# Attention and experts in one program: other blocks' operands stepped at first products only, two weight fetches two steps and one step later

## The chip, the cores and the metric

The kernel runs on one core of a Trainium2 chip. The metric is the device time of one execution in microseconds (us); lower is better. The engines are TensorE (PE, matrix products; its weight loads are PEld), VectorE (DVE), ScalarE (ACT), GpSimd (POOL) and SyncE (SP), which issues most of the transfers.

## The reference

A banded attention feeds a layer of four experts. Heads 0 to 3 look back 32 positions, heads 4 to 7 look back 128 positions in steps of 4. Every token goes through all four experts, weighted by its normalised probabilities.

```python
# q, k, v: (4 batches, 8 heads, 576, 64); x: (2304, 512); w1: (4, 512, 1024); w2: (4, 1024, 512)
scores = scale * np.matmul(q, k.transpose(0, 1, 3, 2))
mask_plain = (rel >= 0) & (rel < window)
mask_dil = (rel >= 0) & (rel < window * dilation) & (rel % dilation == 0)
scores = np.where(masks[None, :, :, :], scores, -1000000000.0)
attn = softmax(scores)
x = np.matmul(attn, v).transpose(0, 2, 1, 3).reshape(B * S, H * D)
p = domain_probs / (domain_probs.sum(-1, keepdims=True) + 1e-09)
for e in range(E):
    h = np.maximum(x @ w1[e], 0.0)
    out += p[:, e:e + 1] * (h @ w2[e])
```

## The kernel before

Everything is fp32. To multiply at the speed of a narrower type, each operand is split into a high part (written by ACT, L113) and the rest (a subtraction on DVE or POOL, L116), and each product is made of three: high by high, rest by high, high by rest.

**The experts.** x is cut into blocks of 384 tokens, numbered i = 0 to 5, and two neighbours make one large block m = 0, 1, 2 of 768 tokens. The 1024 columns of F of each expert are cut into units u of 256 columns. A visit is one pair (u, m); there are 48, some 15.6 us each, and `visits` (L497) lists them: block 0 first, for the units u = 1 to 15, then blocks 1 and 2 for each unit. A visit makes the first product x @ w1 by Strassen-Winograd's scheme, seven products of quarters in place of eight: `mm1_a` (L415) makes two of them and `mm1_b` (L428) five. They need sums of quarters of w1 and of x. Then `mm2` (L463) makes the second product for half 1 of the tokens and afterwards for half 0, three tiles of 128 tokens each; behind every tile DVE adds the weighted tile to `acc` (L488). In between stand two steps of the next visit's `mm1_a`. Banks: `m2` has two for the tiles until the attention is over, then four; `m1x` and `m1y` have one each, then two.

DVE makes L423, L439 and L443 (sums of products), then L406 (the rest parts `hl` of the hidden layer, behind ACT's high parts `hh`, L400), then the three L488 of a half.

**The operands of x.** For a block i, `x_part` (L208) splits one quarter: the high part on ACT, the rest part (`xl_T`, `xl_B`) on POOL if i is even, on DVE if i is odd. `x_sums` (L198) makes the four sums of quarters on DVE, L203, one piece each. They are generators: every piece is one instruction or two.

**The lists.** `queue` holds pieces of the weights and of block 0's x, `later` the pieces of the other blocks' x. `step()` (L569) issues one piece of a list. After each yield of the experts' generator the main loop calls it once or more. `need` (L580) issues all pieces of one kind at once, if they haven't been stepped through yet; so does `need(x_sums, 5)` (L556) in the visit before the last of block 0.

**The attention** is a pipeline of steps of two granules; a granule is one batch, one pair of heads and a third of the sequence. Eight stages run over the granules at different lags, and the experts' visits are woven in behind each step, from step 10 on. SP loads q and k (`q_s`, `k_s`, six buffers each, L245, L246) and the weights (`r`, L98 for w1 and L106 for w2) and, once, the probabilities (`pw`, L737). v is loaded from ACT's queue for the first two batches. `steps` and the fetches at fixed steps (`if n == 4:` and so on) set the order on SP.

Every engine runs its instructions in the order of the program.

Of the kernel before, what the change touches and what calls it, by code (L numbers as in the profile page):

```python
# [21 lines left out]
def band_masks(S):  # L22


    import numpy as np

    masks, which = [], []
    for run in (S, S // DILATION):
        for i in range(S // QB):
            a = (i * QB + np.arange(QB))[:, None]  # L30
            c = (i * QB - WINDOW + np.arange(KB))[None, :]
            seen = (c >= 0) & (a - c >= 0) & (a - c < WINDOW) & (a // run == c // run)
            m = np.where(seen, np.float32(0), np.float32(-8e9))
            same = [j for j, other in enumerate(masks) if np.array_equal(other, m)]
            if not same:
                same = [len(masks)]
                masks.append(m)
            which.append(same[0])
    return np.stack(masks), which
# [3 lines left out]
def kernel(  # L43
# [12 lines left out]
    _, which = band_masks(qT.shape[3])  # L56
    B, NP, _, S = qT.shape
    NT, DM = out.shape
    E, _, F = w1.shape
# [35 lines left out]
    def fetch_w1(u):  # L95
        e, s = divmod(u % NU, FPE)
        r = wp.tile([128, 4, FU], F32, tag="r1", name="r1", bufs=2)
        nc.sync.dma_start(  # L98
            out=r, in_=w1[e, :, s * FU:(s + 1) * FU].rearrange("(c p) f -> p c f", p=128)
        )  # L100
        raw1[u] = r

    def fetch_w2(u):
        e, s = divmod(u % NU, FPE)
        r = wp.tile([128, 2, DM], F32, tag="r2", name="r2")
        nc.sync.dma_start(  # L106
            out=r, in_=w2[e, s * FU:(s + 1) * FU, :].rearrange("(c p) d -> p c d", p=128)
        )
        raw2[u] = r
# [353 lines left out]
    def mm2(k, first, last, half):  # L463
        u, m = k
        e = u // FPE % E
        if first and m not in acc_t:
            if m == NBL - 1:
                pools["late"]()
            acc_t[m] = pools["acc"].tile([128, TB // 128, DM], F32, name=f"acc_{m}")
        for i in range(TH // 128):  # L470
            at = half * (TH // 128) + i
            tt = m * (TB // 128) + at
            acc = acc_t[m][:, at, :]
            po = pools["m2"].tile([128, 512], F32, tag="m2", name="m2")

            cs = range(2) if half == 0 else (1, 0)
            for n, (c, low) in enumerate([(c, low) for low in range(2) for c in cs]):
                h = h_t[k, f"{c + 1}{half + 1}"][low][:, i * 128:(i + 1) * 128]
                for x, w in enumerate(w2_op[u, c][:2 - low]):
                    nc.tensor.matmul(  # L480
                        po, h, w, start=(n == 0 and x == 0), stop=(n == 3)
                    )
            if first:
                nc.vector.tensor_scalar(
                    out=acc, in0=po, scalar1=pn[:, tt, e:e + 1], scalar2=None, op0=ALU.mult
                )
            else:
                nc.vector.scalar_tensor_tensor(  # L488
                    out=acc, in0=po, scalar=pn[:, tt, e:e + 1], in1=acc,
                    op0=ALU.mult, op1=ALU.add,  # L490
                )
            if last:
                nc.sync.dma_start(out=out[tt * 128:(tt + 1) * 128, :], in_=acc)
            yield


    visits = [(u, 0) for u in range(1, NU)]  # L497
# [2 lines left out]
    def experts(begin):  # L500
# [24 lines left out]
        for i, (u, m) in enumerate(visits):  # L525
# [22 lines left out]
            if m == blocks[0]:  # L548
                need(w2_late, u)
            yield from mm2((u, m), *ends, 1)  # L550
            if i + 1 < len(visits):
                begin()
                yield from opening
                if visits[i + 1] == (NU - 1, 0):

                    need(x_sums, 5)  # L556
                    for n in ("T2", "T1"):
                        for j in (4, 5):
                            prepare(x_part, j, n)
            yield from mm2((u, m), *ends, 0)  # L560
            if m == blocks[-1] and u + 2 <= LAST:
                prepare(w2_late, u + 2)
# [3 lines left out]
    queue = []  # L566
    later = []

    def step(of=None):  # L569
        of = queue if of is None else of  # L570
        while of:
            if next(of[0][1], 0) != 0:
                return
            of.pop(0)

    def prepare(what, *args, soon=False, of=None):
        of = queue if of is None else of
        of.insert(0 if soon else len(of), ((what, args), what(*args)))
# [11 lines left out]
    with tc.manual_schedule():  # L590
# [58 lines left out]
        def weigh():  # L649

            nc.vector.reduce_sum(out=ps_, in_=pw, axis=mybir.AxisListType.X)
            nc.vector.tensor_scalar(
                out=ps_, in0=ps_, scalar1=1e-9, scalar2=None, op0=ALU.add
            )
            nc.vector.reciprocal(out=pr_, in_=ps_)
            nc.vector.tensor_tensor(
                out=pn, in0=pw, in1=pr_.to_broadcast([128, NTT, E]), op=ALU.mult
            )
# [17 lines left out]
        def dummies(n):  # L676

            for _ in range(n):
                wt = pools["m2"].tile([128, 512], F32, tag="m2", name="wt")
                nc.tensor.matmul(wt[:, :256], warm[:, :128], warm, start=True, stop=True)  # L680
# [21 lines left out]
        flat = [g for s in steps for g in s]  # L702
        first_x = []
        qk_done = av_done = qk_next = v_next = 0

        dummies(18)
        ffn = experts(begin)
        for n in range(len(steps) + LAG):
            while qk_next < min(qk_done + min(6, 3 + n), len(flat)):
                load_qk(*flat[qk_next])  # L710
                if qk_next == 0:
                    load_masks()
                qk_next += 1
            while v_next < min(av_done + 6, qk_done + 2, len(flat)):
                load_v(*flat[v_next])
                v_next += 1
            for stage, lag in stages:
                if 0 <= n - lag < len(steps):
                    stage(n - lag, steps[n - lag])
            if n < len(steps):  # L720
                qk_done += len(steps[n])
            if n >= LAG:
                av_done += len(steps[n - LAG])
            for i, names in when.get(n, ()):
                for name in names:
                    of = first_x if i < 2 else later
                    if name is None or name == "T2":
                        prepare(x_sums, i, of=of)
                    if name is not None:
                        prepare(x_part, i, name.upper(), of=of)  # L730
            queue[:0] = first_x
            first_x.clear()
            if n == 3:
                fetch_w1(0)
            if n == 4:
                fetch_w2(0)
                nc.sync.dma_start(out=pw, in_=probs.rearrange("(t p) e -> p t e", p=128))  # L737
            if n == 5:
                prepare(w1_split, 0)
            if n == 7:  # L740
                prepare(w2_late, 0)
                fetch_w1(1)
            if n == START + 1:
                weigh()
                prepare(w1_split, 1)
                prepare(w1_sums, 1)
            if n == OPEN - 1:
                prepare(w2_late, 1)
            if n == START + 2:
                fetch_w2(1)  # L750
            if n == OPEN:
                fetch_w1(2)
            if n == OPEN:
                gate.add("open")
            if n < START:
                dummies(4 if n < 4 else 1)
                step()
                if n > 4:
                    step()
                    step()  # L760
                continue
            for _ in range(PACE if "open" in gate else 2):
                if next(ffn) == "idle":
                    dummies(2)
                    for _ in range(3):
                        step()
                    break
                step()
                if len(queue) > 8:
                    step()  # L770
                elif later and len(queue) < 5:
                    step(later)
        gate.add("over")
        for _ in ffn:
            step()
            if len(queue) > 6:
                step()
            step(later)


# [53 lines left out]
```

## Time and profile before

| | |
|---|---|
| time, median of 3 runs | 854.83 us (854.17 to 855.73) |
| the profiled execution | 850.82 us, span 849.0 us |
| PE busy | 828.1 us, 98% of the span |
| DVE busy | 499.9 us, 59% |
| POOL busy | 419.1 us, 49% |
| ACT busy | 327.6 us, 39% |

A share is busy time over the span; an engine with a lower share than the first may still be the one that ends a wait. The first 45 us are attention and loads, the visits with block 0 reach to about 330 us with the attention woven in, and behind that only the experts are left.

### The profile page before, as it was taken

The numbers are of one execution on the slowest core, as the hardware profiler recorded it, in microseconds if no ns is written. First come the engines' busy times: TensorE is split into PE (matmuls) and PEld (weight loads), VectorE is DVE, ScalarE is ACT, GpSimd is POOL, SyncE is SP. The second block draws the span as 40 slices with busy tenths as digits, with TensorE's granted clock in tenths as the row PEclk, the third lists the DMA queues.
The fourth block names the chain that finished last, engine by engine and source line by source line (L and its number), as shares of the span: only waits on it lengthen the run. The fifth ranks groups of instructions, "written<-read, shape, count | busy, mean of one in ns | idle before, by whom it ended". The sixth has DMA issues, their size and how long they took to land.

```text
span 849.0 us, 13445 instructions
## 1 busy us (share of the span) xinstructions
PE 828.1 (98%) x5090; PEld 732.1 (86%) x5090; DVE 499.9 (59%) x1027; ACT 327.6 (39%) x772; POOL 419.1 (49%) x484
## 2 busy tenths in 40 slices
PE   8798999999999999999999999999999999999998
PEld 5577788887898888899899898898998998988986
DVE  4777766669555568655545545555555455455554
ACT  3555454445454355533233233242242242232321
POOL 4677987677676678931432332342341342242210
PEclk9999999999999999999999999999999999999999
DMA  8762322332221222310100100101101001010003
GB/s 234 218 184 73 128 85 84 108 120 64 78 90 51 57 71 72 124 51 26 50 25 25 51 26 26 50 25 38 37 26 50 26 25 49 26 35 17 1 26 124
DMA packets 54528, 56.77 MB, mean 67 GB/s; under 512 B 5952, under 2 KB 43840, under 8 KB 54464
## 3 DMA queue, kind: packets, MB, share of 16 engines
q1 hardware_dynamic: 49472, 52.38, 19.9%
q10 hardware_dynamic: 4992, 3.54, 1.5%
q8 instruction: 40, 0.66, 0.3%
q14 instruction: 24, 0.20, 0.1%
HBM read 51.19 MB, written 4.72 MB: 66 GB/s over the span
## 4 chain that ended last, share of the span: by engine, by line
PE 92%; DVE 3%; DMA 1%; ACT 1%; POOL 1%; issue 1%; SPq 0%; ACTq 0%; POOLq 0%; DVEq 0%
PE m L480 45%; PE m1x L382 24%; PE m1y L382 17%; PE po L349 2%; PE sc L264 2%; PE pt L329 2%; DMA q_s<-qT 1%; PE wt L680 1%; DVE acc L488 1%; DMA k_s<-kT 1%; DVE xl_T L116 1%; DVE hl L406 0%; ACT hh L400 0%; DVE xr L203 0%; DVE s L423 0%
## 5 line engine op out<-in xcount | busy, mean ns | idle before, releaser
L488 DVE SCALAR_TENSOR_TENSOR acc<-m,pn,acc 128x512 f32<-128x512 f32 x270 | 201.9, 749 | 130.9 <-PE m L480 130.7
L480 PE MATMUL m<-w2h,hh 128*128 128x512 f32 x576 | 226.9, 394 | 3.9 <-DVE acc L488 3.2
L480 PE MATMUL m<-w2l,hh 128*128 128x512 f32 x576 | 225.4, 391 | 0.0
L116 POOL TENSOR_TENSOR g2l<-r,g2h 128x256 fp32r<-128x256 f32 x124 | 93.0, 775 | 239.7 <-PE m L480 212.2
L480 PE MATMUL m<-w2h,hl 128*128 128x512 f32 x576 | 178.5, 391 | 0.0
L400 ACT ACTIVATE hh<-s 128x384 fp32r<-128x384 f32 x94 | 49.4, 526 | 248.3 <-DVE s L423 197.8
L480 PEld LDWEIGHTS m<-w2h,hh 128*128 128x128 f32 x576 | 108.1, 188 | 26.8 <-DVE acc L488 6.1
L480 PEld LDWEIGHTS m<-w2h,hl 128*128 128x128 f32 x576 | 108.1, 188 | 24.0 <-DVE hl L406 0.3
L480 PEld LDWEIGHTS m<-w2l,hh 128*128 128x128 f32 x576 | 108.2, 188 | 20.1
L116 POOL TENSOR_TENSOR w2l<-r,w2h 128x512 fp32r<-128x512 f32 x62 | 80.6, 1320 | 45.4 <-ACT w2h L113 45.0
L116 POOL TENSOR_TENSOR g1l<-r,g1h 128x256 fp32r<-128x256 f32 x93 | 68.5, 752 | 66.9 <-ACT g1h L113 66.9
L439 DVE TENSOR_TENSOR s<-m1x,s 128x384 f32<-128x384 f32 x47 | 26.2, 557 | 103.0 <-PE m1x L382 101.3
L432 ACT ACTIVATE u<-m1x 128x384 f32<-128x384 f32 x47 | 23.1, 492 | 144.4 <-PE m1x L382 144.4
L406 DVE SCALAR_TENSOR_TENSOR hl<-s,hh 128x384 fp32r<-128x384 f32 x94 | 60.2, 640 | 28.4 <-ACT hh L400 28.4
L382 PE MATMUL m1x<-xh_T,g2h 128*128 128x384 f32 x156 | 53.1, 340 | 1.8 <-DVE s L423 1.8
L382 PE MATMUL m1x<-xl_T,g2h 128*128 128x384 f32 x156 | 52.9, 339 | 0.0
L382 PE MATMUL m1x<-xh_T,g2l 128*128 128x384 f32 x156 | 52.7, 338 | 0.0
L113 ACT ACTIVATE g2h<-r 128x256 fp32r<-128x256 f32 x125 | 43.4, 405 | 4.4 <-POOL r L145 4.4
L382 PE MATMUL m1y<-xl_B,g2h 128*128 128x384 f32 x128 | 43.0, 336 | 0.0
L382 PE MATMUL m1y<-xh_B,g2h 128*128 128x384 f32 x128 | 43.0, 336 | 0.0
L382 PE MATMUL m1y<-xh_B,g2l 128*128 128x384 f32 x128 | 42.9, 335 | 0.0
L278 DVE CUSTOM_DVE_ANT_0 sm<-sc,mask 128x96 f32<-128x96 f32 x144 | 27.8, 254 | 18.8 <-PE sc L264 17.4
(92 smaller groups left out, 1542.3 us busy)
## 6 DMA issues: line engine op xcount, KB each, us to landing
r<-w SPq DMA_DIRECT2D x64, 512.0 KB, 3.5
k_s<-kT SPq DMA_DIRECT2D x48, 112.0 KB, 3.3
q_s<-qT SPq DMA_DIRECT2D x48, 96.0 KB, 3.4
out<-acc SPq DMA_DIRECT2D x18, 256.0 KB, 2.0
v_s<-vw ACTq DMA_DIRECT2D x24, 144.0 KB, 4.1
v_s<-vw SPq DMA_DIRECT2D x24, 144.0 KB, 3.2
mask<-masks SPq DMA_DIRECT2D x1, 288.0 KB, 4.6
pw<-probs SPq DMA_DIRECT2D x1, 36.0 KB, 5.9
```

Of the source, the lines that this page charges most:

```text
L113: nc.scalar.activation(out=hi, in_=src, func=AF.Copy)
L116: lo_eng.tensor_tensor(out=lo, in0=src, in1=hi.bitcast(F32), op=ALU.subtract)
L264: nc.tensor.matmul(banks[swap][o, i * KB:(i + 1) * KB], q_s[h, c0:c0 + QB], k_s[h, c0:c0 + KB], start=True, stop=True, skip_group_check=True,)
L278: nc.vector.tensor_tensor_reduce(out=sm[:, k * GB + i, :KB], in0=banks[k][:, i * KB:(i + 1) * KB], in1=mask[:, which[blk if p < NP // 2 el ...
L329: nc.tensor.transpose(pt[:KB, i * 128:(i + 1) * 128], sm[:, k * GB + i, :KB], ident)
L382: nc.tensor.matmul(bank, w[:, k], x[:, k], start=(first and k == 0 and i == 0), stop=(last and k == 1 and i == 2), skip_group_check=True,)
L400: nc.scalar.activation(out=hi, in_=src, func=AF.Relu)
L406: nc.vector.scalar_tensor_tensor(out=lo, in0=src, scalar=0.0, in1=hi.bitcast(F32), op0=ALU.max, op1=ALU.subtract)
L432: nc.scalar.activation(out=u2, in_=x, func=AF.Copy)
L439: nc.vector.tensor_tensor(out=s5, in0=x, in1=s5, op=ALU.add)
L480: nc.tensor.matmul(po, h, w, start=(n == 0 and x == 0), stop=(n == 3))
L488: nc.vector.scalar_tensor_tensor(out=acc, in0=po, scalar=pn[:, tt, e:e + 1], in1=acc, op0=ALU.mult, op1=ALU.add,)
```

## The change

It has three parts. (In the diff the first lines are those of `mm2`.)

1. q and k are loaded six granules ahead from the first step, where it were three, four and five.
2. The first fetch of w2 and the load of the probabilities move from step 4 to step 6; the splits of w2's first unit and the second fetch of w1 move from step 7 to step 8.
3. `mm2` yields "acc" behind each of its tiles, and the list `later` is stepped only behind yields that are not "acc", that is behind the pieces of the first products; in the main loop the limit on the length of `queue` below which it is stepped rises from 5 to 8.

```diff
-            yield
+            yield "acc"
...
-            while qk_next < min(qk_done + min(6, 3 + n), len(flat)):
+            while qk_next < min(qk_done + 6, len(flat)):
...
-            if n == 4:
+            if n == 6:
                 fetch_w2(0)
                 nc.sync.dma_start(out=pw, in_=probs.rearrange("(t p) e -> p t e", p=128))
             if n == 5:
                 prepare(w1_split, 0)
-            if n == 7:
+            if n == 8:
                 prepare(w2_late, 0)
                 fetch_w1(1)
...
-                if next(ffn) == "idle":
+                at = next(ffn)
+                if at == "idle":
...
                 step()
                 if len(queue) > 8:
                     step()
-                elif later and len(queue) < 5:
+                elif at != "acc" and len(queue) < 8:
                     step(later)
         gate.add("over")
-        for _ in ffn:
+        for at in ffn:
             step()
             if len(queue) > 6:
                 step()
-            step(later)
+            if at != "acc":
+                step(later)
```

TensorE's order is the same row by row. On DVE, ACT and POOL the order differs in the start and at three places of the visits. The first fence shows SP in the start, before: the fetch of w1 (`r_299`), two pairs of q and k, then w2 (`r_360`) and the probabilities.

```order
L98 DMA r_299<-w 128x4x256
L245 DMA q_s<-qT 128x192
L246 DMA k_s<-kT 128x224
L245 DMA q_s<-qT 128x192
L246 DMA k_s<-kT 128x224
L106 DMA r_360<-w 128x2x512
L737 DMA pw<-probs 128x18x4
L245 DMA q_s<-qT 128x192
L246 DMA k_s<-kT 128x224
```

The same stretch of SP after the change, from the pairs of q and k that now stand ahead of w2 (`r_495`).

```order
L245 DMA q_s<-qT 128x192
L246 DMA k_s<-kT 128x224
L245 DMA q_s<-qT 128x192
L246 DMA k_s<-kT 128x224
L106 DMA r_495<-w 128x2x512
L737 DMA pw<-probs 128x18x4
L245 DMA q_s<-qT 128x192
L246 DMA k_s<-kT 128x224
```

Four pairs that stood behind w2 and the probabilities stand ahead of them now.

The next fence shows DVE at the place that the texts call B, in one visit of block 0, where block 3's operands are made; before.

```order
L488 SCALAR_TENSOR_TENSOR acc_983<-m_2758,pn,acc_983 128x512
L116 TENSOR_TENSOR xl_B_1_1528<-xr,xh_B_1_1527 128x2x192
L203 TENSOR_TENSOR xr<-xr 128x2x192 x2
L439 TENSOR_TENSOR s_2775<-m1x,s_2775 128x384
L203 TENSOR_TENSOR xr<-xr 128x2x192
L443 TENSOR_TENSOR u_2774<-m1y,u_2774 128x384
L406 SCALAR_TENSOR_TENSOR hl<-s_2775,hh 128x384
L406 SCALAR_TENSOR_TENSOR hl<-u_2774,hh 128x384
L203 TENSOR_TENSOR xr<-xr 128x2x192
L406 SCALAR_TENSOR_TENSOR hl<-m1x,hh 128x384
L116 TENSOR_TENSOR xl_T_1_1594<-xr,xh_T_1_1593 128x2x192
L488 SCALAR_TENSOR_TENSOR acc_983<-m_2846,pn,acc_983 128x512
```

And after the change, the same visit on DVE.

```order
L488 SCALAR_TENSOR_TENSOR acc_983<-m_2754,pn,acc_983 128x512
L116 TENSOR_TENSOR xl_B_1_1478<-xr,xh_B_1_1477 128x2x192
L116 TENSOR_TENSOR xl_B_1_1493<-xr,xh_B_1_1492 128x2x192
L439 TENSOR_TENSOR s_2769<-m1x,s_2769 128x384
L116 TENSOR_TENSOR xl_B_1_1507<-xr,xh_B_1_1506 128x2x192
L443 TENSOR_TENSOR u_2768<-m1y,u_2768 128x384
L406 SCALAR_TENSOR_TENSOR hl<-s_2769,hh 128x384
L406 SCALAR_TENSOR_TENSOR hl<-u_2768,hh 128x384
L203 TENSOR_TENSOR xr<-xr 128x2x192
L406 SCALAR_TENSOR_TENSOR hl<-m1x,hh 128x384
L203 TENSOR_TENSOR xr<-xr 128x2x192 x2
L488 SCALAR_TENSOR_TENSOR acc_983<-m_2843,pn,acc_983 128x512
```

Two splits stand ahead of L439 now, and from L439 to the acc there are four pieces in place of three.

The last two fences show DVE at place C, where the sums of blocks 4 and 5 are made, in front of the last visit of block 0; before, and then after.

```order
L423 TENSOR_TENSOR s_4162<-m1x,s_4162 128x384
L406 SCALAR_TENSOR_TENSOR hl<-s_4162,hh 128x384
L203 TENSOR_TENSOR xr<-xr 128x2x192
L488 SCALAR_TENSOR_TENSOR acc_983<-m_4226,pn,acc_983 128x512
L488 SCALAR_TENSOR_TENSOR acc_983<-m_4238,pn,acc_983 128x512
L488 SCALAR_TENSOR_TENSOR acc_983<-m_4252,pn,acc_983 128x512
L439 TENSOR_TENSOR s_4263<-m1x,s_4263 128x384
```

After the change seven sums in a row stand where one stood.

```order
L423 TENSOR_TENSOR s_4159<-m1x,s_4159 128x384
L406 SCALAR_TENSOR_TENSOR hl<-s_4159,hh 128x384
L203 TENSOR_TENSOR xr<-xr 128x2x192 x7
L488 SCALAR_TENSOR_TENSOR acc_983<-m_4226,pn,acc_983 128x512
L488 SCALAR_TENSOR_TENSOR acc_983<-m_4238,pn,acc_983 128x512
L488 SCALAR_TENSOR_TENSOR acc_983<-m_4252,pn,acc_983 128x512
L439 TENSOR_TENSOR s_4263<-m1x,s_4263 128x384
```

The other six stood one by one between the rows of this visit's half 1 and ahead of L423.

## Rows read from the trace of the kernel before

**Rows 1.** Page, busy time of each engine, share of the span, instructions.

```profile
PE 828.1 (98%) x5090; PEld 732.1 (86%) x5090; DVE 499.9 (59%) x1027; ACT 327.6 (39%) x772; POOL 419.1 (49%) x484
```

**Rows 2.** Stretches: length, busy PE, PEld, DVE, ACT, POOL, granted clock, DMA share, GB/s.

```profile
20.00:40.00 20.00, 14.64 (x255) 11.24 (x253) 15.19 (x74) 12.27 (x34) 12.53 (x12) 0.91 0.82 216
330.00:800.00 470.00, 470.00 (x2350) 425.24 (x2350) 253.98 (x401) 157.48 (x362) 174.46 (x212) 1.00 0.12 39
```

**Rows 3.** TensorE's timeline, start: start, length, instruction, idle time before and releaser.

```profile
27.75 1.22 PE L264 MATMUL sc<-k_s,q_s 64*64 64x96 f32 x20 [1.40 <-ACT xr L365]
...
37.04 0.71 PE L264 MATMUL sc<-k_s,q_s 64*64 64x96 f32 x20 [1.22 <-ACT xr L365]
```

**Rows 4.** SyncE's timeline in the start.

```profile
17.49 0.47 SPq L737 DMA_DIRECT2D pw<-probs  x1
18.93 3.61 SPq L245 DMA_DIRECT2D q_s<-qT  x1
```

**Rows 5.** ScalarE's timeline in the start.

```profile
27.14 0.55 ACT L365 ACTIVATE xr<-po 128x192 f32<-128x192 f32 x2 [3.95 <-issue]
...
31.51 0.55 ACT L365 ACTIVATE xr<-po 128x192 f32<-128x192 f32 x2 [1.16 <-PE pt L329]
...
36.30 0.69 ACT L365 ACTIVATE xr<-po 128x192 f32<-128x192 f32 x2 [2.40 <-DMA k_s<-kT]
```

**Rows 6.** Page, transfers: count, KB each, median us from issue to landing.

```profile
k_s<-kT SPq DMA_DIRECT2D x48, 112.0 KB, 3.3
```

**Rows 7.** VectorE's timeline in the start, a split of w2.

```profile
30.84 1.63 DVE L116 TENSOR_TENSOR w2l<-r,w2h 128x512 fp32r<-128x512 f32 x1
```

**Rows 8.** Timeline at place A, DVE and TensorE.

```profile
96.10 1.07 DVE L203 TENSOR_TENSOR xr<-xr 128x384 f32<-128x384 f32 x1
...
97.89 0.50 PE L480 MATMUL m<-w2h,hh 128*128 128x512 f32 x1 [1.89 <-DVE acc L488]
```

**Rows 9.** Timelines at place B and the visit before, DVE and TensorE.

```profile
178.19 0.56 DVE L439 TENSOR_TENSOR s<-m1x,s 128x384 f32<-128x384 f32 x1 [2.46 <-PE m1x L382]
...
182.66 0.75 DVE L488 SCALAR_TENSOR_TENSOR acc<-m,pn,acc 128x512 f32<-128x512 f32 x1 [0.44 <-PE m L480]
...
196.71 0.56 DVE L439 TENSOR_TENSOR s<-m1x,s 128x384 f32<-128x384 f32 x1
...
201.72 0.74 DVE L488 SCALAR_TENSOR_TENSOR acc<-m,pn,acc 128x512 f32<-128x512 f32 x1
...
205.51 1.52 DVE L116 TENSOR_TENSOR xl_T<-xr,xh_T 128x384 fp32r<-128x384 f32 x1
...
211.75 0.50 PE L480 MATMUL m<-w2h,hh 128*128 128x512 f32 x1 [1.27 <-DVE acc L488]
```

**Rows 10.** Chain that ended last, at place C: start, length, piece.

```profile
327.30 1.06 PE m1x L382 x6
...
336.68 1.04 PE m1x L382 x6
...
338.76 4.12 PE m L480 x18
```

**Rows 11.** VectorE's timeline at place C.

```profile
330.84 0.55 DVE L423 TENSOR_TENSOR s<-m1x,s 128x384 f32<-128x384 f32 x1
...
333.48 2.06 DVE L488 SCALAR_TENSOR_TENSOR acc<-m,pn,acc 128x512 f32<-128x512 f32 x3
335.74 0.56 DVE L439 TENSOR_TENSOR s<-m1x,s 128x384 f32<-128x384 f32 x1 [0.21 <-PE m1x L382]
```

**Rows 12.** Line L203, all sums: ns min/median/max, first and last start.

```profile
L203 DVE TENSOR_TENSOR xr<-xr x24: 542/725/1127, 48.2 to 332.5; 128x384 f32<-128x384 f32 x24
```

**Rows 13.** Timeline ahead of place C, DVE and TensorE.

```profile
319.63 0.67 DVE L116 TENSOR_TENSOR xl_B<-xr,xh_B 128x384 fp32r<-128x384 f32 x1 [2.03 <-ACT xh_B L113]
...
320.82 0.44 PE L382 MATMUL m1x<-xh_T,g1h 128*128 128x384 f32 x1 [0.50 <-DVE s L439]
```

**Rows 14.** GpSimd's timeline at place C.

```profile
332.33 2.52 POOL L116 TENSOR_TENSOR g2l<-r,g2h 128x256 fp32r<-128x256 f32 x3 [1.94 <-ACT g2h L113]
```

## The prediction

> **What bounds the kernel now.** I read the busy shares first [rows 1]: TensorE is busy 98% of the span, and the next engine, VectorE (DVE), 59%. The split into stretches then shows where the missing 2% lie [rows 2]: from 330 to 800 us TensorE is busy 470.00 of 470.00 us, while from 20 to 40 us it is busy 14.64 of 20 at a mean granted clock of 0.91. No instruction of TensorE is added, removed or moved by this change. So it can only move the waits of TensorE in the first 340 us, and each is found in TensorE's timeline by the bracket behind a row: 1.40 and 1.22 us in the start [rows 3], and 1.89, 1.27 and 0.50 us where TensorE waits for DVE at three places of the visits, A, B and C below. These add up to 6.28 us, and that is about what all of them together could ever give. The profiled execution took 850.82 us, 4.01 below the median of the runs (854.83); I add my changes to the median, as changes in waits carry over.
>
> **Part 1, the start: fetches moved past the loads of q and k.** In SyncE's timeline [rows 4] pw is issued at 17.49; the load of q behind it is issued from 18.93 to 22.54, so pw costs the queue 22.54 − 17.49 = 5.05 us. The attention step that needs this q and k is late: ScalarE (ACT) stands still for 3.95 us before its row of 27.14 [rows 5], and the scores of TensorE behind it wait 1.40 [rows 3]. With the fetch two steps later, the four pairs of q and k that stood behind it load before it, and this wait goes. What is late next is the pair behind pw's new place. By my estimate pw is then issued at 22.3 us, one step of 4.4 to 4.8 later [rows 5] (the step's loads wait for buffers, so the place in the order sets the time only this roughly). With 5.05 us for pw, q and k of the next pair are issued by 27.4, and 3.3 us, the median of k's loads [rows 6], bring them to 30.7. The ACT row that stands behind that load comes about 0.5 later (such a row's own length), at 31.2. Without the first wait that row would stand at 31.51 − 1.40 = 30.1. So 1.1 of the 1.40 comes back and 0.3 is gained. The second wait (ACT's row of 36.30, which stands 2.40 for want of a k [rows 5], and 1.22 on TensorE [rows 3]) has the fetch of w1 in front, which moves behind two more pairs. But now both splits of w2 on DVE stand in one step ahead of its row sums; one took 1.63 [rows 7]. I let 0.9 of the 1.22 stay and count 0.3 gained. Together −0.6. The bounds: both waits gone and the slow stretch too is −4.4 (2.62, and 9% of the 20 us at a granted clock of 0.91, 1.8 us; the twenty score matmuls took 1.22 at the one place and 0.71 at the other [rows 3]). On the other side, nothing gained and a further split of 1.2 in front: +1.2. I stand near the lower gain because pw goes with its whole cost to another place of the same queue.
>
> The third edit of the start, six pairs ahead from the first step, moves nothing: SyncE's rows up to the first w1 are the same in both orders. It is free.
>
> **Part 2, place A (92 to 106 us), block 2's sums.** TensorE's wait of 1.89 ends with the first acc of DVE; ahead of it stands one sum (L203) of 1.07 [rows 8]. That sum stays where it is; the sums between the accs and the one ahead of L423 go behind the accs. I count −0.2, with bounds of −0.4 (half the sum ahead of L423) and +0.4 (half a sum, now ahead of L443).
>
> **Part 3, place B (186 to 214 us), block 3.** Here the order shows what the rule does: the pieces that stood between accs, where DVE had time, now stand at the first products. From L439 to the end of the first acc DVE took 5.22 us without pieces (178.19 to 182.66, and 0.75), 0.44 of it idle, so 4.78 of its own work; with three pieces between them it took 5.75 (196.71 to 201.72, and 0.74) [rows 9]. With pieces at the sums' median of 0.73 [rows 12] that leaves 3.56 for its own work; the visits differ, and I take it between these, at 4.2. TensorE asks for the bank of the first acc at its third tile: 5.77 after L439 (338.76 and two thirds of 4.12, minus 335.74 [rows 10, 11]). After the change four pieces stand there. At 0.73 each that is 4.2 + 2.9 = 7.1, and TensorE waits 1.4; with the shortest, 0.54, and 3.56 it is 5.7 and no wait, with 0.73 and 4.78 it is 7.7 and 1.9. Ahead of L439 two splits xl_B now stand. Just that, a split that waited 2.03 for ACT, cost TensorE 0.50 at 320.82 [rows 13], and I count 0.5 here (0 to 0.5), and as much in the next visit, where two xl_T stand in the same place. In half 0 the split of 1.52 at 205.51 goes, from which the wait of 1.27 came [rows 9], but a sum of 0.73 stands directly ahead of the acc, as at place A. There I count 0.9 (0.5 to 1.3), and 0.1 for the one xl_T ahead of the next acc (0 to 0.5). In sum 0.5 + 1.4 + 0.9 + 0.5 + 0.1 − 1.27 = +2.1; the bounds are −0.8 and +3.4.
>
> **Part 4, place C (312 to 340 us), blocks 4 and 5.** The wait of 0.50 [rows 13] goes, as no split waits ahead of L439 any more: −0.5. But the eight sums of these blocks are no longer fed one by one, and all that are left are forced at once: seven in a row ahead of the accs of half 0. They start at about 329.7 (the product ends at 327.30 + 1.06, less the 0.5 gained; then 1.7 for L423 and hl as from 330.84 on, and 0.1 between [rows 10, 11]). Behind them stand three accs (2.06) and L439 (0.56), and TensorE asks for L439's bank at 336.68 − 0.5 = 336.2 [rows 10, 11]. That leaves 3.9 us for the seven, 0.56 for each. A sum took 0.54 at least, 0.73 in the median and 1.13 at most [rows 12]; the long ones lie beside work of GpSimd (POOL), and POOL has three splits there from 332.33 on [rows 14]. I take 0.8, 5.6 in all, so 1.7 us of wait (0 to 4.0). C is +1.2, between −0.5 and +3.5.
>
> One page of the Trainium skill bears on this: "SBUF — State Buffer", section "Who interferes with whom", says that VectorE and GpSimd share one pair of ports and that whoever has it locks the other out. By the trace the lock is not complete: sums took up to 1.13 us beside POOL instead of 0.54, where three POOL splits took 2.52 in a row. By the Trainium skill's page each sum would wait for one whole split, which is rival (c) with +6.6 in place of +2.5.
>
> **The sum:** −0.6 − 0.2 + 2.1 + 1.2 = +2.5 us, so 857.3.
>
> **The rivals.**
> (a) *The start gives all of its waits.* For it: the four pairs do load earlier, and the second wait has w1 in front of it. Against it: pw costs its 5.05 us in the new place too. Then −2.6 − 0.2 + 2.1 + 1.2 = +0.5, 855.3.
> (b) *The pieces fit, and the kernel is faster.* Mechanism: where POOL stands idle, a sum takes 0.54. Then four pieces in B end before TensorE asks, and the seven in C take 3.8, under the 3.9 that there are; it is decided at 0.56 for a piece. For it: the shortest of the 24 sums [rows 12]. Against: the median of 0.73, and POOL's splits from 332.33 [rows 14]. It gives −0.6 − 0.2 − 0.8 − 0.5 = −2.1, 852.7.
> (c) *Each sum waits for a whole POOL split.* Splits are 0.84 each [rows 14], so a sum costs 1.38, seven 9.7, that is 5.8 over; C is +5.3, and B perhaps +2.1 as before. The sum is +6.6, 861.4. Against it: no sum of before took more than 1.13 [rows 12]. It is the lock of the Trainium skill's page above, taken in full.
> (d) *Nothing to be measured.* The burst costs about 1.2 net, and B comes out at nothing because the pieces use DVE's idle times: −0.6 − 0.2 + 0 + 1.2 = +0.4, 855.2.
>
> **How the numbers follow.** Changes below 0.2%, 1.7 us, can't be told from none by a measurement of this kernel. The forecast has a chance of 0.46, (a) 0.18, (b) 0.18, (c) 0.06, (d) 0.12. Faster by more than 0.2% holds (b), 0.18. Within it lie (a) and (d), 0.30. Slower is the forecast and (c), 0.52. The median forecast's own range is 856.6 to 859.5. The range reaches down to (b) at 852.7, and a little below, 852.4, since the start could give somewhat more; upwards to 861.0, where (c) is left out and the upper bounds of B and C (+1.3 and +2.3 above my values) are in.
>
> **What would show it.** The step on the start is right if the ACT row after 3.95 us of idle time is gone and a shorter wait stands near 31 us; if TensorE has no wait above 0.5 from 20 to 40, (a) holds. B is right if TensorE waits at the third tile of half 1 near 199 to 203 us for acc, and 0.5 at A22's product for L439. C is right if seven sums stand in a row on DVE near 330 us, with 0.8 each, and TensorE waits for L439 behind them. If their mean is under 0.56, (b) holds, if over 1.3, (c). I would be wrong if a new wait of one of these kinds were followed by a stretch at a lower granted clock, which no row here prices, or if the waits lay in a place where no order moved.

## The result: slower by 0.95%

The changed kernel took 863.83 us in the median of 7 executions (859.60 to 867.55), the kernel before 855.14 (853.98 to 856.06): a ratio of 1.0095, with a 95% interval of 1.0066 to 1.0125. Measured once more it was 863.34, 1.0081 (1.0067 to 1.0094). I had said 857.3, and up to 861.0.

The page of the changed kernel, its busy times, answers to [rows 1].

```profile
span 859.3 us, 13445 instructions
...
PE 831.8 (97%) x5090; PEld 734.1 (85%) x5090; DVE 502.3 (58%) x1027; ACT 326.8 (38%) x772; POOL 417.7 (49%) x484
```

The shares fell by a point or less, and the number of instructions is the same: nothing was added, something waits. Its timeline shows where TensorE does, from the start to place C (start, length, instruction, and in brackets the idle time before it and what ended that). Waits that the kernel before has in the same way, as 2.42 at 64.24 and 1.83 at 80.66, are left out.

```profile
21.37 0.71 PE L264 MATMUL sc<-k_s,q_s 64*64 64x96 f32 x20 [0.93 <-ACT xr L365]
...
31.57 1.23 PE L264 MATMUL sc<-k_s,q_s 64*64 64x96 f32 x20 [2.44 <-ACT xr L365]
...
91.92 0.50 PE L480 MATMUL m<-w2h,hl 128*128 128x512 f32 x1 [0.56 <-DVE hl L406]
...
100.43 0.50 PE L480 MATMUL m<-w2h,hh 128*128 128x512 f32 x1 [1.45 <-DVE acc L488]
...
200.60 0.45 PE L382 MATMUL m1x<-xh_T,g1h 128*128 128x384 f32 x1 [0.62 <-DVE s L439]
...
208.06 0.50 PE L480 MATMUL m<-w2h,hh 128*128 128x512 f32 x1 [2.32 <-DVE acc L488]
...
218.30 0.50 PE L480 MATMUL m<-w2h,hh 128*128 128x512 f32 x1 [0.78 <-DVE acc L488]
...
224.76 0.45 PE L382 MATMUL m1x<-xh_T,g1h 128*128 128x384 f32 x1 [0.62 <-DVE s L439]
...
346.66 0.45 PE L382 MATMUL m1x<-xh_T,g1h 128*128 128x384 f32 x1 [3.42 <-DVE s L439]
```

The rows of 100.43 and 218.30 are the instructions of 97.89 [rows 8] and 211.75 [rows 9]: by them the changed kernel is 2.54 and then 6.55 us behind. At the end it is 10.3 behind (859.3 against 849.0). So place B up to its half 0 cost about 4, and what comes behind, mostly place C, the rest. The first 2.54 come from ahead of place A; in the profiled execution of the kernel before the start was quick (experiment 7). Before C's wait the 0.50 of [rows 13] is gone, as forecast.

VectorE's timeline at place B shows what the wait of 2.32 is for: two sums that take 2.84 us. GpSimd's timeline, in the second fence, has two splits of w2 beside them that take 2.83.

```profile
203.02 1.09 DVE L203 TENSOR_TENSOR xr<-xr 128x384 f32<-128x384 f32 x1
204.03 0.55 DVE L406 SCALAR_TENSOR_TENSOR hl<-m1x,hh 128x384 fp32r<-128x384 f32 x1
204.50 2.84 DVE L203 TENSOR_TENSOR xr<-xr 128x384 f32<-128x384 f32 x2
207.26 1.40 DVE L488 SCALAR_TENSOR_TENSOR acc<-m,pn,acc 128x512 f32<-128x512 f32 x2
```

```profile
204.10 2.83 POOL L116 TENSOR_TENSOR w2l<-r,w2h 128x512 fp32r<-128x512 f32 x2 [0.41 <-ACT w2h L113]
```

The same at place C: VectorE, then GpSimd.

```profile
336.18 0.91 DVE L406 SCALAR_TENSOR_TENSOR hl<-s,hh 128x384 fp32r<-128x384 f32 x1 [0.59 <-ACT hh L400]
337.01 7.14 DVE L203 TENSOR_TENSOR xr<-xr 128x384 f32<-128x384 f32 x7
344.08 2.06 DVE L488 SCALAR_TENSOR_TENSOR acc<-m,pn,acc 128x512 f32<-128x512 f32 x3
346.06 0.54 DVE L439 TENSOR_TENSOR s<-m1x,s 128x384 f32<-128x384 f32 x1
```

```profile
335.94 3.78 POOL L116 TENSOR_TENSOR g2l<-r,g2h 128x256 fp32r<-128x256 f32 x4
339.67 3.08 POOL L116 TENSOR_TENSOR g1l<-r,g1h 128x256 fp32r<-128x256 f32 x3
```

Seven sums take 7.14 us, 1.02 each, beside these splits and two sums of GpSimd's that follow at 342.83 and 343.82. With 3.9 us free for them, that is 3.2 too much, and TensorE waits 3.42.

The granted clock by stretches (length, busy times, clock, DMA share, GB/s) shows a second cost: behind the wait of 2.32 TensorE runs at the lower of its two levels, 1.2 GHz.

```profile
208.00:212.00 4.00, 3.94 (x30) 2.83 (x30) 2.03 (x4) 0.00 (x0) 1.03 (x1) 0.57 0.65 204
346.00:353.00 7.00, 6.34 (x31) 5.60 (x32) 5.21 (x10) 5.59 (x13) 3.85 (x4) 1.00 0.11 40
```

Behind the 3.42 the clock stayed at the full level in this execution; in the next profile of the same kernel it did not:

```profile
345.00:353.00 8.00, 6.34 (x19) 5.88 (x20) 4.21 (x8) 3.92 (x9) 2.92 (x4) 0.57 0.01 2
```

### The profile page after: what moved, and what is told of

It is laid out like the page before. It is cut to its first block, busy times and chain, and to the rows that moved or that the text cites. A ratio compares the mean times of both kernels' runs of the same rounds, so it can differ in the third digit from the quotient of the medians.

```text
span 859.3 us, 13445 instructions
## 1 busy us (share of the span) xinstructions
PE 831.8 (97%) x5090; PEld 734.1 (85%) x5090; DVE 502.3 (58%) x1027; ACT 326.8 (38%) x772; POOL 417.7 (49%) x484
## 4 chain that ended last, share of the span: by engine, by line
PE 87%; DVE 5%; DMA 3%; ACT 2%; POOL 1%; issue 1%; SPq 0%; ACTq 0%; DVEq 0%; POOLq 0%
PE m L480 44%; PE m1x L382 23%; PE m1y L382 16%; DVE xr L203 2%; PE po L349 1%; DMA v_s<-vw 1%; PE pt L329 1%; PE sc L264 1%; DVE hl L406 1%; DMA pw<-probs 1%; DMA q_s<-qT 1%; DVE acc L488 1%; DMA k_s<-kT 1%; ACT hh L400 0%; DVE sm L278 0%
## 5 line engine op out<-in xcount | busy, mean ns | idle before, releaser
L439 DVE TENSOR_TENSOR s<-m1x,s 128x384 f32<-128x384 f32 x47 | 26.2, 557 | 98.9 <-PE m1x L382 97.6
```

What stands on the lines that cost most here:

```text
L439: nc.vector.tensor_tensor(out=s5, in0=x, in1=s5, op=ALU.add)
```

## Experiments

**1. The rule for the lists alone, and the start alone.** My theory after the result was that the places B and C make the loss, and the rival that the start and the clock do.

```diff
 # e1_steps: the kernel before, with
+            yield "acc"
...
+                elif at != "acc" and len(queue) < 8:
+                    step(later)
...
+            if at != "acc":
+                step(later)
 # e2_fetch: the kernel before, with
+            while qk_next < min(qk_done + 6, len(flat)):
...
+            if n == 6:
                 fetch_w2(0)
...
+            if n == 8:
                 prepare(w2_late, 0)
```

> The kernel before with only the rule for the list of the other blocks (part 3); the start as before. Theory P (places): the cost sits at places B and C, where the profile of the changed kernel shows TensorE waiting for VectorE 0.62 + 2.32 + 0.78 + 0.62 and 3.42 us; then this kernel alone takes +7 to +8 us against before, 862 to 863. Rival S (start): the moved fetches and the stretches at half the clock behind their waits make most of it; then it takes less than +4.

Measured: 862.70, 1.0094 (1.0072 to 1.0116). The theory held; the waits at B and C are the same to 0.01 us, and the wait of 3.42 at 346.32 is followed by a stretch at half the clock.

> The kernel before with only parts 1 and 2 (loads of q and k six ahead, two fetches moved back); the lists as before. Theory P: the start costs +1 us and, where a stretch at half the clock follows a wait, up to +3: 856 to 858, with no new wait at places B and C. Rival S: +5 or more. My sum before the result had -0.6 for it.

Measured: 853.58, 0.9989 (0.9975 to 1.0004). Both lines were wrong; the start is no loss. On top of the rule for the lists it gave nothing either: 863.83 and 863.34 with it, 862.70 without (e1_steps). Before's first profile had an execution with a quick start (850.82, while its runs are at 855), so differences of two single profiles in the start mislead.

**2. Which place.** The changed kernel with the loop behind the attention as before, so that C's sums are fed singly; and the kernel before with only that loop changed, so that only C's row of sums comes.

```diff
 # e3_tail: the changed kernel, with
-            if at != "acc":
-                step(later)
+            step(later)
 # e8_burst: the kernel before, with the reverse of this edit alone
```

> The changed kernel, but behind the end of the attention the list is stepped after every yield as before, so that the sums of blocks 4 and 5 are fed one by one again at place C. Theory P: the row of seven sums (7.14 us) is gone and with it the wait of 3.42 us; -2.9 us against the changed kernel, about 861, with place B unchanged at +5. Rival: VectorE has too much to do at place C in any order, and the wait returns behind the accs or at the next visit; then less than -1.

Measured: 857.32, 1.0028 (1.0012 to 1.0045), 6.5 and 6.0 less than the changed kernel's two medians; the 861 that I expected held the waits alone. The sums' wait is gone and the 0.50 is back; B's four waits stand unchanged. It gave back more than the waits: where a stretch at half the clock follows them, it goes too.

> The kernel before with the new rule only behind the end of the attention, so that place C is that of the changed kernel (seven sums in a row) and places A and B are those of before. Theory: TensorE's wait of 3.42 for L439 comes, and the 0.50 goes; +2.9 us, and up to +2.8 more in those executions in which a stretch at half the clock follows the wait (345.7 to 352.9 us in the kernel with part 3 alone), so 858 to 860. Rival: the loss of 6.5 us between the changed kernel and the one without the row of sums came from elsewhere; then less than +2.

Measured: 859.34, 1.0047 (1.0033 to 1.0060) against 855.88: +3.5 to +4. TensorE's timeline has the wait:

```profile
343.63 0.69 PE L382 MATMUL m1x<-xh_T,g1h 128*128 128x384 f32 x1 [3.42 <-DVE s L439]
```

The length of 0.69 in place of 0.45 is the half clock. From the row behind this wait to the end it takes 512.6 us in the changed kernel's first profile, whose clock stayed at the full level there, and 513.9 to 515.4 in the four others with the wait (e11_limit5, e8_burst, after_again, e1_steps). So C costs 2.9 in waits and 1.3 to 2.8 for the clock, where it falls.

**3. What a sum costs.** Here GpSimd has nothing to do beside the seven sums: the weights' pieces are held back, and ACT's next split needs the sixth sum.

```diff
 # e6_hold: the changed kernel, with
+            if (u, m) == (NU - 2, 0):
+                gate.add("hold")             # ahead of mm2 half 1
...
-                            prepare(x_part, j, n)     # behind need(x_sums, 5)
+                            prepare(x_part, j, n, soon=n == "T2" and j == 5)
+                    need(x_part, 5, "T2")
+                    gate.discard("hold")
...
+            if "hold" not in gate:           # around step() of the loop
```

> The changed kernel, but the pieces of the weights are held back from half 1 of the second products ahead of place C until the seven sums are through, and ACT first splits one quarter that needs the sixth sum, so that GpSimd has nothing to do beside the sums. Theory L (a sum beside a GpSimd instruction costs what the GpSimd instruction leaves): the seven sums take 0.47 to 0.56 each, 3.3 to 3.9 in a row in place of 7.14, and TensorE's wait of 3.42 for L439 falls below 0.7; the weights' pieces are late instead, so the time as a whole may come out anywhere from -5 to +3. Rival: seven sums in a row cost 1 us each by themselves; then they still take about 7.

Measured: 864.78, 1.0119 (1.0093 to 1.0146). The time is what the late weights cost (TensorE waits 3.09 for g2h and 2.00 for g2l). The sums are what it was for; VectorE, then GpSimd:

```profile
333.97 4.06 DVE L203 TENSOR_TENSOR xr<-xr 128x384 f32<-128x384 f32 x7
```

```profile
329.84 0.93 POOL L147 TENSOR_TENSOR r<-r 128x256 f32<-128x256 f32 x1
338.65 2.50 POOL L116 TENSOR_TENSOR w2l<-r,w2h 128x512 fp32r<-128x512 f32 x2 [7.88 <-ACT w2h L113]
341.12 2.78 POOL L116 TENSOR_TENSOR g2l<-r,g2h 128x256 fp32r<-128x256 f32 x4
```

GpSimd stands from 330.8 to 338.65, and the seven sums take 4.06, 0.58 each, in place of 7.14. The rival (a row of sums costs 1 us each by itself) is out. ACT stands for most of this row as well, but it isn't ACT's work that made the sums long: in the kernel before, those of 49.11 and 54.12 us, with ACT at work and GpSimd idle, took 0.54. The wait for L439 is gone, though under cover of the others.

**4. One sum less at place B.** With the old limit of 5 one of the two sums ahead of the first acc goes to the next visit.

```diff
 # e11_limit5: the changed kernel, with
-                elif at != "acc" and len(queue) < 8:
+                elif at != "acc" and len(queue) < 5:
```

> The changed kernel with the limit on the queue at 5 as before, in place of 8. On VectorE one of the two sums between the last hl and the first acc of place B goes to the next visit, ahead of L439. Theory: that sum took 1.42 of the 2.32 us that TensorE waits there; the wait falls to about 0.9 and is followed by no stretch at half the clock, while the next visit's wait of 0.62 grows by up to 0.6: -1 to -3 us against the changed kernel, 861 to 862.5. Rival: the price of place B doesn't depend on that one sum, since VectorE is late from L439 on; the wait stays over 2 us and the time the same.

Measured: 858.69, 1.0054 (1.0037 to 1.0071) against 853.85, about 3.9 less than the changed kernel's +8.7 and more than the 1 to 3 that I expected. TensorE's wait there, and the clock behind it:

```profile
207.55 0.50 PE L480 MATMUL m<-w2h,hh 128*128 128x512 f32 x1 [0.78 <-DVE acc L488]
```

```profile
206.00:214.00 8.00, 7.22 (x77) 5.57 (x76) 6.03 (x20) 2.05 (x6) 4.92 (x5) 1.00 0.31 102
```

The sum was worth 1.54 of wait, and with it the stretch at half the clock is gone: from this row to the acc's wait of half 0 it takes 8.76 us (to 216.31), where the changed kernel takes 10.24 (208.06 to 218.30). So the clock cost 1.5 there. Part of the rest lies at place A, whose wait before the acc is also gone in this order. With the old limit the waits at A and B (0.56, 0.62, 0.78, 0.79 and 0.50) come to 3.25, where the kernel before has 3.16 (1.89 and 1.27): there the rule lost by the raised limit, and what is left of the loss is for the most part place C (experiment 2).

**5. The opposite rule.** The kernel before, where the list is stepped only at the tiles of the second products while the attention runs.

```diff
 # e4_acc: the kernel before, with "acc" as yield of mm2, and
-                elif later and len(queue) < 5:
+                elif at == "acc" and len(queue) < 5:
```

> The kernel before with the opposite rule: while the attention runs, the list is stepped only behind yields that are acc, that is at the tiles of the second products. Theory P (first products are the places without slack): TensorE's waits of 1.89 at place A and 1.27 at place B shrink, -1 to -3 us against before, 852 to 854. Rival: pieces between the accs hold the banks of the tiles as long as pieces ahead of them do; then the waits stay or grow, and it takes as long as before or +1 to +3.

Measured: 851.67, 0.9962 (0.9946 to 0.9978): faster by 0.4%. At A the wait of 1.89 is gone, a new one of 0.53 stands at 121.19, and at B it is 0.82:

```profile
208.74 0.50 PE L480 MATMUL m<-w2h,hh 128*128 128x512 f32 x1 [0.82 <-DVE acc L488]
```

These waits are 1.8 us less together. With A's wait goes what the clock does behind it: in three of four profiles with this wait (before_again, e2_fetch, e8_burst; not in the first of the kernel before) a stretch at half the clock follows, and from A's row to B's it takes 115.3 to 115.4 us there, 113.86 without it.

**6. The start, on top of the opposite rule.** Parts 1 and 2 of the change; or only the probabilities at step 10; or both.

```diff
 # e7_acc_fetch: e4_acc with the edits of e2_fetch
 # e9_acc_pw: e4_acc with
-                nc.sync.dma_start(out=pw, in_=probs.rearrange("(t p) e -> p t e", p=128))
...
+            if n == START:
+                nc.sync.dma_start(out=pw, in_=probs.rearrange("(t p) e -> p t e", p=128))
 # e10_all: both
```

> The kernel before with the opposite rule (list stepped at acc only while the attention runs) and with parts 1 and 2 of the change. Theory: the two small gains add, -3.5 and -1.6, 850 (849 to 851.5). Rival: the fetches moved back have no gain of their own, and it takes the 851.7 of the opposite rule or more.

Measured: 848.88, 0.9936 (0.9915 to 0.9957), a little under the expected range.

> The kernel before with the opposite rule, and the load of the probabilities alone moved from step 4 to step 10 (w2 stays at step 4). Theory: what makes q and k late in the start is the 3.6 to 3.9 us that SyncE stands at the issue behind the probabilities; then TensorE's wait near 27 us goes without coming back at 31, and it takes 849 to 850.5. Rival: the fetch of w2 or the transfers as a whole are what makes them late, and it takes 851.7 as without the move.

Measured: 848.48, 0.9928 (0.9909 to 0.9948). The time is 0.5 below the expected range, and the reason isn't the one that I gave: TensorE still waits 1.88 before its row of 26.78.

> The opposite rule, parts 1 and 2, and the probabilities at step 10. Theory: both stalls of the start are gone, 848 to 850, below all the others. Rival: the probabilities are late for the weighting at step 11, VectorE stands there and TensorE behind it: 852 or more.

Measured: 848.48, 0.9926 (0.9906 to 0.9946), no more than either alone. With no probabilities in the start at all, the stall stands at 30.45, as in TensorE's and ACT's timelines:

```profile
30.45 0.71 PE L264 MATMUL sc<-k_s,q_s 64*64 64x96 f32 x20 [3.16 <-ACT xr L365]
```

```profile
29.84 0.55 ACT L365 ACTIVATE xr<-po 128x192 f32<-128x192 f32 x2 [3.34 <-DMA v_s<-vw]
```

What ends it is a load of v. So the probabilities are not what makes the start late, or not alone. These three can't be told apart; they are the fastest of all, 0.6 to 0.7% below the kernel before.

**7. The scatter.** Both kernels profiled once more.

> The kernel before, unchanged, profiled once more: its first profile took 850.82 us, 4 us below the median of its runs. Theory: the difference lies in the first 100 us, in more or longer stretches at half the clock and other waits in the start, and the waits from 180 us on are those of the first profile (1.27, 0.50).

The kernel before took 855.04 this time (span 853.2), and from 180 us on it has the waits of the first profile to 0.02 (1.29 and 0.51). The 4.2 us of difference arise before 110 us. The mean granted clock is 0.988 in place of 0.994: over the span that is short of the full clock by 10.2 us in this execution and by 5.1 in the first.

> The changed kernel once more, for its scatter (859.6 to 867.6 in seven runs). Theory: the waits at places B and C return to 0.1 us (0.62, 2.32, 0.78, 0.62, 3.42); what changes from execution to execution is the first 100 us and which of the waits is followed by a stretch at half the clock. Median 861 to 865.

Measured: 863.34, 1.0081 (1.0067 to 1.0094); B's and C's waits returned (0.62, 2.32, 0.79, 0.62, 3.42). Between these two typical executions the spans differ by 8.8 us, like the medians. The place A row stands at 100.81 and 100.58 (−0.2), that of B at 216.11 and 218.38 (+2.3, so 2.5 from A to B), and what is left, 6.5, comes behind: C's wait, the end of B's, and the clock. The 2.5 are what is left when the stretch at half the clock behind A's row, which only the kernel before has here, is set off; against the first profile of the kernel before, which has none, it was 4.

## Why the prediction was wrong

**The direction was right, the size wrong by a factor of 3.5.** The waits came at the places of B and C that the prediction named, and by the mechanism that it named; what was mis-sized were these two terms, and what the clock does behind their waits had no term.

*The start, −0.6.* Right within what can be told: −1.6 alone (ratio 0.9975 to 1.0004), nothing on top of the rule, 2.8 on top of the opposite rule (851.67 and 848.88). That the first wait goes and comes back near 31 us was right (31.57), though with 2.44 where I took 1.1. In the changed kernel's trace the queue does what I worked out: the probabilities are issued at 22.98 (I took 22.3), the issue of q behind them ends at 27.41 (27.4 for the pair), and ACT's row, which a q releases, stands at 30.97 (31.2). SyncE, then ACT:

```profile
22.98 0.48 SPq L737 DMA_DIRECT2D pw<-probs  x1
23.56 3.85 SPq L245 DMA_DIRECT2D q_s<-qT  x1
```

```profile
30.97 0.55 ACT L365 ACTIVATE xr<-po 128x192 f32<-128x192 f32 x2 [3.71 <-DMA q_s<-qT]
```

But a stall stands at this place without the probabilities as well (experiment 6), so moving them doesn't remove it.

*Place A, −0.2.* The first acc's wait is 1.45 in place of 1.89, but in both profiles of the changed kernel 0.56 or 0.55 for hl stands ahead of it: nothing gained, nothing lost in waits. The clock gained: a stretch at half of it follows the wait of 1.85 to 1.88 in three of four profiles, and costs 1.4 (experiment 5); it follows that of 1.44 to 1.46 in none of five.

*Place B, +2.1.* Its four terms measured 0.62 for L439 (I took 0.5), 2.32 for the first acc (1.4), 0.78 for half 0 (0.9), 0.62 in the next visit (0.5), less 1.27. That is +3.1 in waits, within the bounds that I gave for the place. The term that failed is the first acc's, over its own upper value of 1.9: the two sums there cost 1.42 each in the mean, not the median of 0.73, with splits of w2 beside them. On top comes the clock: in all five profiles with the 2.32 (the changed kernel's two, e1_steps, e3_tail, e6_hold) a stretch of some 3.4 us at half the level follows, which cost 1.5 us. In the one that stood at 0.78 there it does not. I had named it as a thing that would make me wrong and said that no row prices it. The trace of the kernel before had such a row: behind the wait of 1.84 at 77.53, which the list of 6.28 us left out, TensorE ran at half the clock, as the stretch from 80 to 81 shows.

```profile
80.00:81.00 1.00, 1.00 (x5) 0.88 (x5) 0.91 (x1) 0.83 (x4) 1.00 (x2) 0.50 0.64 140
```

*Place C, +1.2.* I took 0.8 for each of the seven sums, from all sums of the kernel before. They took 1.02, because GpSimd was at work beside all seven of them: +2.9 in waits, again inside the bounds, and then the clock: four of five profiles with the 3.42 (3.43 in e11_limit5) have a stretch at the lower level, of 3.4 or 6.8 us, which cost 1.3 to 2.8.

So the step that failed is the price of a sum: it was read off a median over places with and without GpSimd's work, while in the changed kernel the sums that end the waits at B and C have GpSimd's work beside all of them. The kernel before shows the price that was to be had: of its seven sums at place C from 323.52 to 332.46, five took 0.98 to 1.10 beside GpSimd's work, the two others 0.54 and 0.62. Two of the five:

```profile
327.23 0.99 DVE L203 TENSOR_TENSOR xr<-xr 128x384 f32<-128x384 f32 x1
...
328.80 0.99 DVE L203 TENSOR_TENSOR xr<-xr 128x384 f32<-128x384 f32 x1
```

The second step that failed is the clock, which the sum put at nothing. Rival (c) had a higher price for a sum, too high at C (1.38 for 1.02) and near the two sums at B (1.42), where it left the term as it was. That its time of 861.4 was the nearest of all is luck: its +5.3 at C is all waits, where the runs have 2.9 and the clock.

The page of the Trainium skill, "SBUF — State Buffer", section "Who interferes with whom", states the reason: a VectorE instruction with two inputs from SBUF contends with a GpSimd one that reads there. The runs bear out the contention: a sum costs 0.58 alone, 1.02 and 1.42 beside GpSimd's work. They don't show one side blocked for the other's whole instruction: alone, the seven sums take 4.06 us, and seven splits would take 4.9 by my estimate (2.78 for four [e6_hold's GpSimd rows]), 9.0 one after the other. The seven sums, with about as much of GpSimd's work beside them, took 7.1. Both sides got longer, a split from 0.70 to about 1.

Experiment 5 speaks against the idea of the change: the opposite rule gains 3.5. My explanation is that pieces at the tiles of the second products lie where VectorE waits for TensorE, while at the first products VectorE makes hl and the sums on which TensorE's next bank depends; no run shows it by itself. Nor is the rule alone the loss: with the old limit it costs next to nothing in waits at A and B (experiment 4), and most of the rest is the row of sums at C.

Two things stay open. Why a wait of 2.32 was followed by the lower clock every time, one of 1.27 to 1.29 and those of 0.8 never, that of 1.85 to 1.89 at place A in three of four, and the 3.42 in four of five, the runs don't tell. And in the start I can't say which transfer is the one that is late.

## What to carry to other kernels

Price an instruction from the rows that stand beside the same work of the other engine, not from a median over the kernel. Try a helper's instruction where its engine waits for the bottleneck (here behind a tile of an accumulation), and not where the bottleneck waits for that engine. Count a wait of some microseconds on TensorE with what the clock does behind it.

## What was not expected of the hardware

A wait of 2.32 us on TensorE was followed by 3.4 us at half the clock in five of five profiles, one of 1.27 to 1.29 us in none of four; 1.5 us came to the 3.1 of waits at place B from this. And two profiles of one unchanged kernel differ by 4.2 us, all of it in the first 110 us, while all waits behind 180 us repeat to 0.02 us.
